# Attention with sinks and a two-matrix gate on one core: a sink tile staged in the gate's buffer, and every piece in a fixed order

## The chip, the cores and the metric

The kernel runs on one core of a Trainium2 chip. The metric is the device time of one execution in microseconds (us), and the reported time is the median over runs. An engine here is one of five: TensorE (PE, with its weight loads shown apart as PEld), VectorE (DVE), ScalarE (ACT), GpSimd (POOL) and SyncE (SP), which only issues DMAs. Each engine works through its own instructions in the order in which they are written; between engines there are semaphores.

## The reference, cut to what matters

```python
scores = matmul(q, k.T) / sqrt(64)                 # batch 4, heads 8, sequence 768, head size 64
keep = (pos_k < n_sink) | ((0 <= pos_q - pos_k) & (pos_q - pos_k < window))   # 4 sinks, window 128
a = softmax(where(keep, scores, -1e9));  x = matmul(a, v)      # -> 3072 tokens x 512
h = x @ w_in                                       # 512 -> 2048
out = (h - tanh(h)) @ w_out                        # 2048 -> 512
```

All inputs are float32. The two matrices come as 64-bit words from which the kernel decodes float32 on the chip.

## The kernel before, in words

The 3072 tokens are cut into 12 chunks of 256 queries (three per batch). The first three chunks are the first ones of batches 0, 1 and 2. Per chunk there are four **units** (a pair of heads each), so 48 units. A unit needs: loads of keys and queries; scores (`products`, L532 for the first twelve units, L539 after them), twice, for two tiles t of 128 queries; `merge` on DVE (L554, L556), which reads the scores out of PSUM; `exponent` on ACT (L564); `sums` on DVE (L584, L585) and `scale` on ACT (L590), which divide; `sinks` on POOL (L599 to L601); and `transposes` on PE (L624) into the PSUM bank t, which ACT (L631) and DVE (L638) copy out into `pts`. When two units (in the first two chunks) or four are done, `attend` makes x of them: `sink_rows` (L665) transposes the sinks' columns, ACT copies them (`sink_copy`, L672), and `values` (L681 with the sinks' values `vsink`, L687 with v) accumulates x, which ACT and DVE split into a high and a low part (L704, L708).

The sinks' values of a batch are made by `sink_values`, seven times in all, whenever the batch changes from one chunk to the next: a DMA (L460) into the tile `vraw`, a rounding copy on ACT into `vsink` (L466), a subtraction and a scaling on POOL in place in `vraw` (L470, L471), and a sum on DVE into `vsink` (L475).

The two matrix products follow in **steps** n = 0 to 95, one for a chunk and an eighth g of the 2048 columns: `first_half(n)` (24 products, L823) makes h; the gate takes tanh on ACT into `gbuf` (L854), the difference on DVE (L857), and a high and a low part (L860, L863; in the later chunks sums and L873, L876); `second_half(n)` multiplies with the second matrix (L905; in the later chunks L939). The weights are decoded once, early: DVE takes three instructions per matrix part (L157, L159, L161), ACT rounds (L747), DVE makes the low part (L751). From step 24 on the first matrix is streamed back from a scratch copy in DRAM into the tiles `ring` and `spare` (L808).

All of this is entered as 3002 **pieces** into one object, `work`: each with its engine, an expected duration, a due time, the function that issues its instructions, and the names that it reads and writes. `Work.order` (L195 to L231) then runs a list scheduler on these numbers: an engine takes, of its ready pieces, the one with the earliest due time. The pieces are issued in the order of their starts in this plan. So the plan fixes only who stands before whom in each engine's queue; the chip's semaphores decide when a piece starts.

## Time and profile before

| what | us |
|---|---|
| median of three runs | 668.6 (666.87 to 668.98) |
| the profiled execution | 670.4 |
| its span, first to last instruction | 668.6 |
| PE busy in it | 650.5 |

The profiled execution is 1.8 us longer than its own span; that part lies outside the instructions. The page's list of engines gives the busy time per engine over the span; windows give the same for a stretch, with the clock that TensorE was granted (1.00 is 2.4 GHz, 0.50 is 1.2 GHz); a timeline gives instructions in order of time, and in brackets how long the engine had stood idle before one and what ended that.

### The profile page before, as it was taken

How to read it: one execution, taken by the hardware profiler on the slowest of the kernel's cores; microseconds unless marked ns; L12 is line 12 of the kernel's file. 1: busy time of each engine (PE TensorE's matmuls, PEld its weight loads, DVE VectorE, ACT ScalarE, POOL GpSimd, SP SyncE). 2: the span in 40 equal slices, each digit the busy share in tenths (PEclk: the TensorE clock that was granted, in tenths of full speed). 3: DMA queues.
4: the chain of work that ended last, by engine and by line, in shares of the span. 5: the costliest groups of instructions: out<-in, count | busy, mean ns of one | idle time of the engine just before them, and what ended most of it. 6: DMA issues, size and time to landing. Idle time of an engine off the chain costs nothing.

```text
span 668.6 us, 14547 instructions
## 1 busy us (share of the span) xinstructions
PE 650.5 (97%) x5099; PEld 603.3 (90%) x5099; DVE 543.8 (81%) x1399; ACT 396.9 (59%) x1024; POOL 164.2 (25%) x331
## 2 busy tenths in 40 slices
PE   6989999999999999999999999999999999999996
PEld 4668899999979899898999999999999999999995
DVE  6889999964999878578798899887899899855654
ACT  5987444345898667567665575676566566523321
POOL 5453100000873232243331212312213212100100
PEclk9899999999999999999999999999999999999999
DMA  5877788884999667899977767767776867656771
GB/s 172 279 254 273 260 268 308 292 289 143 226 212 279 217 205 226 236 291 279 287 221 219 223 208 239 251 185 209 243 221 203 266 182 209 206 165 210 259 199 40
DMA packets 79502, 152.97 MB, mean 229 GB/s; under 512 B 9596, under 2 KB 25852, under 8 KB 79420
## 3 DMA queue, kind: packets, MB, share of 16 engines
q1 hardware_dynamic: 65900, 121.52, 58.3%
q0 software_dynamic: 13376, 30.30, 16.1%
q8 instruction: 42, 0.69, 0.4%
q14 instruction: 40, 0.33, 0.1%
q10 hardware_dynamic: 144, 0.13, 0.1%
HBM read 131.47 MB, written 20.45 MB: 227 GB/s over the span
## 4 chain that ended last, share of the span: by engine, by line
PE 76%; DVE 8%; ACT 6%; DMA 4%; issue 2%; POOL 2%; SPq 0%; POOLq 0%; DVEq 0%; ACTq 0%
PE h L823 33%; PE s L939 10%; PE o L939 7%; PE o L905 6%; PE x L687 3%; PE s L905 3%; PE t L624 2%; PE t L687 2%; DMA kraw<-kp 2%; PE t L539 2%; PE t L905 2%; PE x L905 2%; PE x L539 1%; ACT p L590 1%; DVE pt L638 1%
## 5 line engine op out<-in xcount | busy, mean ns | idle before, releaser
L823 PE MATMUL h<-xall,ring 128*128 128x256 f32 x990 | 130.3, 279 | 0.0
L823 PEld LDWEIGHTS h<-xall,ring 128*128 128x128 f32 x990 | 121.1, 188 | 1.4 <-issue 0.7
L854 ACT ACTIVATE gbuf<-h 128x512 f32<-128x512 f32 x96 | 57.1, 595 | 91.4 <-PE h L823 67.6
L823 PE MATMUL h<-xall,spare 128*128 128x256 f32 x738 | 97.6, 279 | 0.0
L873 ACT CAST ghbuf<-gbuf 128x896 fp32r<-128x896 f32 x55 | 51.7, 940 | 68.5 <-DVE gbuf L870 68.4
L823 PEld LDWEIGHTS h<-xall,spare 128*128 128x128 f32 x738 | 90.9, 188 | 0.5
L370 POOL DMA_DIRECT2D qraw<-qd x36 | 26.6, 740 | 255.8 <-DVE q L511 199.9
L876 DVE TENSOR_TENSOR glbuf<-gbuf,ghbuf 128x896 fp32r<-128x896 f32 x55 | 60.0, 1090 | 20.4 <-ACT ghbuf L873 17.5
L564 ACT ACTIVATE p<-p,st 128x132 f32<-128x132 f32 x132 | 52.4, 399 | 12.9 <-DVE st L556 12.0
L857 DVE TENSOR_TENSOR gbuf<-h,gbuf 128x512 f32<-128x512 f32 x55 | 37.9, 689 | 22.9 <-ACT gbuf L854 22.4
L905 PE MATMUL o<-w,ghbuf 128*128 128x512 f32 x192 | 49.9, 395 | 0.2 <-ACT ghbuf L860 0.2
L823 PEld LDWEIGHTS h<-xall,w 128*128 128x128 f32 x384 | 46.9, 188 | 2.0 <-DVE w L751 0.4
L823 PE MATMUL h<-xall,w 128*128 128x256 f32 x384 | 48.2, 279 | 0.2 <-DVE w L751 0.2
L502 DVE TENSOR_TENSOR ks<-kraw,ks 64x392 fp32r<-64x392 f32 x72 | 40.4, 561 | 5.9 <-ACT ks L497 3.8
L590 ACT ACTIVATE p<-p,st 128x132 f32<-128x132 f32 x132 | 42.6, 395 | 3.1 <-DVE st L585 2.6
L905 PEld LDWEIGHTS o<-w,ghbuf 128*128 128x128 f32 x192 | 33.8, 188 | 6.1 <-ACT ghbuf L860 0.5
L857 DVE TENSOR_TENSOR h<-h,gbuf 128x512 f32<-128x512 f32 x41 | 28.5, 696 | 13.0 <-ACT gbuf L854 12.7
L497 ACT CAST ks<-kraw 64x392 fp32r<-64x392 f32 x72 | 37.1, 515 | 2.2 <-DMA kraw<-kp 1.3
L860 ACT CAST ghbuf<-h 128x512 fp32r<-128x512 f32 x41 | 24.0, 585 | 21.1 <-DVE h L857 20.4
L939 PE MATMUL s<-edge,ghbuf 128*128 128x256 f32 x220 | 35.3, 279 | 0.0
L939 PE MATMUL o<-w,ghbuf 128*128 128x256 f32 x220 | 35.1, 278 | 0.0
L939 PE MATMUL s<-w,ghbuf 128*128 128x256 f32 x220 | 35.1, 278 | 0.0
(185 smaller groups left out, 1546.5 us busy)
## 6 DMA issues: line engine op xcount, KB each, us to landing
ring<-wscr SPq DMA_DIRECT2D x165, 256.0 KB, 4.8
spare<-wscr SPq DMA_DIRECT2D x123, 256.0 KB, 4.7
qraw<-qd POOLq DMA_DIRECT2D x36, 256.0 KB, 5.2
wraw<-w_in SPq DMA_DIRECT2D x16, 512.0 KB, 5.8
wraw<-w_out SPq DMA_DIRECT2D x16, 512.0 KB, 5.6
wscr<-w SPq DMA_DIRECT2D x16, 512.0 KB, 7.4
kraw<-kp POOLq DMA_DIRECT2D x36, 196.0 KB, 4.7
v<-vp POOLq DMA_DIRECT2D x18, 256.0 KB, 3.8
```

What stands on the lines that cost most here:

```text
L497: nc.scalar.copy(ks[u][r, h, :], kt[u][r, :])
L502: (nc.gpsimd if KP else nc.vector).tensor_tensor(k[o, h, :], t[r, :], k[r, h, :].bitcast(F32), op=ALU.subtract)
L564: nc.scalar.activation(e, e, AF.Exp, bias=st[u][:, j : j + 1], scale=-1.0, accum_out=st[u][:, 4 + j : 5 + j],)
L590: nc.scalar.activation(pr[u][:, j, :], pr[u][:, j, :], AF.Copy, scale=s[:, 8 + j : 9 + j])
L687: nc.tensor.matmul(xps[key][(p - p0) // 2][h * 64 : h * 64 + 64, p % 2, a:z], lhsT=vt[cc, i][:, hd : hd + D], rhs=rhs, start=False, stop=p ...
L823: nc.tensor.matmul(hps[n][:, f, :], lhsT=w, rhs=x, start=r == 0, stop=r == 11)
L854: nc.scalar.activation(g0, h(), AF.Tanh)
L857: nc.vector.tensor_tensor(g0 if strassen(n) else h(), h(), g0, op=ALU.subtract)
L873: nc.scalar.copy(ghbuf[:, n % 2], gbuf[:, 1:, :])
L876: nc.vector.tensor_tensor(low7(n), gbuf[:, 1:, :], ghbuf[:, n % 2].bitcast(F32), op=ALU.subtract)
L905: nc.tensor.matmul(sums_of(n, cc, t), lhsT=a[:, f, t * P : (t + 1) * P], rhs=wt[1, g][:, (0, 1, 0)[i], f, :], start=first and not low and ...
L939: nc.tensor.matmul(acc, lhsT=a[:, b, :], rhs=factor(g, m, part % 2), start=g == 0 and part == 0 and m in (4, 1, 2, 7), stop=closes(n) and ...
```

## The change: what it does

Four edits. **The order** of the 3002 pieces is no longer planned: it is a permutation, stored as a compressed string, and `Work.order` unpacks it and asserts that no piece stands before one that it depends on. **The staging**: `sink_values` of batch 1 (the second batch; it is made twice, for the second and for the sixth chunk) uses the first 128 columns of the gate's tile `gbuf` in place of `vraw`, and the name that orders it is the gate's, `"gr"`. **The names**: the copies of the transposes into `pts` now also name the decode buffers that lie in the same memory (`"dw"`), so that the assertion sees them. **ASIDE**: in five steps the low part of the gate's numbers lies at element 4 of its tile, in steps 81, 84, 87, 90 and 93, where it lay at 4 or 44 in steps 81, 83, 86, 89 and 92; all other steps keep 48.

```diff
-    WAKE = {"PE": 250, "ACT": 170, "DVE": 90, "POOL": 100, "SP": 80}
-    def __init__(self, slack, pad, late, land):
+    ORDER = (
+        "c-jrt0|OW~69CZUF1brCwQbwBZQHhO+qP|Et8KemyVb^4uHW~5#nVcuu?o}#WtCGwO;M4QQBl=6HD8TaG1NqbYLX)5)eOaIvYM$D"
...
     def order(self):
-        todo = {}
...
-        return sorted(start, key=lambda n: (start[n], n)), start
+        todo = [n for n, in iter_unpack("<H", decompress(b85decode(self.ORDER)))]
+        at = {n: i for i, n in enumerate(todo)}
+        assert len(at) == len(todo) == len(self.all)
+        assert all(at[a] < at[n] for n in todo for a in self.all[n][4])
+        return todo
...
-        ASIDE = {81: 4, 83: 44, 86: 4, 89: 44, 92: 4}
+        ASIDE = {n: 4 for n in (81, 84, 87, 90, 93)}
...
         def sink_values(b, due):
-            slot = "vraw"
+            slot = "gr" if b == 1 else "vraw"
+            raw_at = gbuf[:, 0, :] if b == 1 else vraw
             def load():
-                nc.sync.dma_start(vraw, vs[32 * b : 32 * b + 32].rearrange("r (p c) -> p r c", c=P))
+                nc.sync.dma_start(raw_at, vs[32 * b : 32 * b + 32].rearrange("r (p c) -> p r c", c=P))
...
-                    nc.scalar.copy(vsink[r, i, :], vraw[r])
+                    nc.scalar.copy(vsink[r, i, :], raw_at[r])
...
-                work.add("ACT", 260, d + 1400, whole, ["t"], [("pt whole", m)])
-            work.add("DVE", 430 if c == 0 else 710, d + 1500, lambda: part(1, below), ["t"], [("pt own", m)])
+                work.add("ACT", 260, d + 1400, whole, ["t"], [("pt whole", m)] + [("dw", m - 2)] * (m > 1))
+            free = [("dw", m - 2)] * (m > 1)
+            work.add("DVE", 430 if c == 0 else 710, d + 1500, lambda: part(1, below), ["t"], [("pt own", m)] + free)
```

What the permutation does to the queues: the first halves keep their order among themselves, the second halves keep theirs, and 33 of the 864 pieces of both stand at another place among the others. From step 86 on (608 us in the profile) PE's queue is the same piece for piece. The attention's pieces move: against the queue before, about one in seven of PE's pieces, and about four in ten of DVE's and ACT's, have another rank among their engine's. Three places follow; line numbers of the changed kernel are some 35 higher (L568 is L532 before, L660 is L624, L702 is L665, L718 is L681, L942 is L905, L575 is L539, L496 is L460).

**PE's queue at the start**, before and then now: `pt` holds keys and queries of units 0 and 1, `kraw,qraw` those of unit 2, `qk` of the later ones; s and o are the PSUM banks of the scores.

```order
L532 MATMUL s_250<-pt 128x260
L532 MATMUL s_251<-pt 128x260
L532 MATMUL o_252<-pt 128x260
L532 MATMUL o_253<-pt 128x260
L532 MATMUL s_250<-kraw_272,qraw_270 128x260
L532 MATMUL s_251<-kraw_272,qraw_270 128x260
L532 MATMUL o_252<-kraw_272,qraw_270 128x260
L532 MATMUL o_253<-kraw_272,qraw_270 128x260
L624 MATMUL t<-ident,p_284 128x128 x4
```

```order
L568 MATMUL s_250<-pt 128x260
L568 MATMUL s_251<-pt 128x260
L660 MATMUL t<-ident,p_291 128x128 x4
L568 MATMUL o_252<-pt 128x260
L568 MATMUL o_253<-pt 128x260
L568 MATMUL s_250<-kraw_304,qraw_276 128x260
L568 MATMUL s_251<-kraw_304,qraw_276 128x260
L568 MATMUL o_252<-kraw_304,qraw_276 128x260
L568 MATMUL o_253<-kraw_304,qraw_276 128x260
```

The four transposes of unit 0 stood behind the scores of unit 2; they now stand behind the first scores of unit 1 and ahead of its second ones.

**SP's queue at the start**, before and then now, from the first DMA behind the branch: `vs` are the sinks' values, `qd` queries, `kp` keys, `vp` values, `w_in` a weight part.

```order
L361 DMA kraw_272<-kp 128x392
L105 DMA qraw_270<-qd 64x256 x2
L405 DMA v_0_289<-vp 128x512
L405 DMA v_1_291<-vp 128x512
L361 DMA qk_287<-kp 128x392
L105 DMA qk_287<-qd 64x256 x2
L460 DMA vraw<-vs 128x1x128
L416 DMA wraw_0_340<-w_in 128x1024
L361 DMA qk_297<-kp 128x392
L105 DMA qk_297<-qd 64x256 x2
```

```order
L496 DMA vraw<-vs 128x1x128
L105 DMA qraw_276<-qd 64x256 x2
L396 DMA kraw_304<-kp 128x392
L396 DMA qk_280<-kp 128x392
L396 DMA qk_282<-kp 128x392
L105 DMA qk_280<-qd 64x256 x2
L451 DMA wraw_0_327<-w_in 128x1024 x2
L105 DMA qk_282<-qd 64x256 x2
L440 DMA v_0_352<-vp 128x512
L440 DMA v_1_354<-vp 128x512
```

The sinks' values of batch 0 are now the first load, and the values of v come behind the keys and queries of units 3 and 4.

**PE's queue at the fourth chunk's x** (190 us), before and then now: `glbuf` is the low part of a gate, `z` the sinks' columns, `zr` their copies.

```order
L624 MATMUL t<-ident,p_2147 128x128 x4
L905 MATMUL o_252<-w_6_1522,glbuf 128x512 x2
L905 MATMUL o_253<-w_6_1522,glbuf 128x512 x2
L665 MATMUL x<-ident,z 128x128 x2
L539 MATMUL s_250<-ks_2225,q_2204 128x260 x2
L539 MATMUL s_251<-ks_2225,q_2204 128x260 x2
L681 MATMUL x<-zr,vsink 128x512
```

```order
L660 MATMUL t<-ident,p_2134 128x128 x4
L702 MATMUL x<-ident,z 128x128 x2
L942 MATMUL o_252<-w_6_1540,glbuf 128x512 x2
L575 MATMUL s_250<-ks_2171,q_2164 128x260 x2
L575 MATMUL s_251<-ks_2171,q_2164 128x260 x2
L942 MATMUL o_253<-w_6_1540,glbuf 128x512 x2
L718 MATMUL x<-zr,vsink 128x512
```

The transposes of the sinks' columns moved ahead of a pair of products with the gate's low part, so that four more products stand between them and the product that reads `zr`.

## Rows read from the trace of the kernel before

**Rows 1.** The page's first part: busy us, share of the span, instructions.
```profile
PE 650.5 (97%) x5099; PEld 603.3 (90%) x5099; DVE 543.8 (81%) x1399; ACT 396.9 (59%) x1024; POOL 164.2 (25%) x331
```
**Rows 2.** Windows: length, busy us (count) of PE, PEld, DVE, ACT, POOL; clock; DMA.
```profile
0.00:60.00 60.00, 50.60 (x292) 38.28 (x293) 48.19 (x206) 46.97 (x173) 30.22 (x77) 0.97 0.73 235
60.00:190.00 130.00, 129.76 (x862) 117.55 (x861) 109.80 (x185) 69.36 (x146) 23.98 (x36) 1.00 0.80 255
190.00:460.00 270.00, 268.15 (x2175) 249.78 (x2174) 227.53 (x631) 180.62 (x484) 81.29 (x159) 1.00 0.79 236
460.00:610.00 150.00, 150.00 (x1339) 146.52 (x1338) 124.73 (x317) 83.77 (x203) 26.03 (x56) 1.00 0.70 212
```
**Rows 3.** PE's timeline in the first 50 us: start, length, what, [idle before it].
```profile
8.11 1.12 PE L532 MATMUL s<-pt 128*128 128x260 f32 x4
...
13.70 1.12 PE L532 MATMUL s<-qk 128*128 128x260 f32 x4 [0.81 <-DMA qk<-qd]
14.65 1.04 PE L532 MATMUL o<-qk 128*128 128x260 f32 x4
17.99 2.07 PE L532 MATMUL s<-qk 128*128 128x260 f32 x4 [2.30 <-DVE nswi L556]
...
49.15 1.77 PE L823 MATMUL h<-xall,w 128*128 128x256 f32 x12
```
**Rows 4.** SP's timeline: issues of the sinks' values, and the issue between them.
```profile
11.19 0.67 SPq L460 DMA_DIRECT2D vraw<-vs  x1
...
15.48 1.11 SPq L105 DMA_DIRECT2D qk<-qd  x2
19.16 0.58 SPq L460 DMA_DIRECT2D vraw<-vs  x1
```
**Rows 5.** ACT's timeline from 9 to 16 us.
```profile
9.79 0.19 ACT L564 ACTIVATION_READ_ACCUMULATOR p<-p,st 128x1 f32 x1
...
10.71 1.29 ACT L590 ACTIVATE p<-p,st 128x132 f32<-128x132 f32 x4
...
15.32 0.62 ACT L466 CAST vsink<-vraw 64x128 fp32r<-64x128 f32 x2 [1.76 <-DMA vraw<-vs]
```
**Rows 6.** DVE's timeline, at 10 to 17 us and at 69 us.
```profile
10.24 0.16 DVE L584 TENSOR_SCALAR st<-st 128x4 f32<-128x4 f32 x1
...
16.88 0.29 DVE L584 TENSOR_SCALAR st<-st 128x4 f32<-128x4 f32 x1 [1.72 <-ACT wide L564]
...
68.80 0.71 DVE L475 SCALAR_TENSOR_TENSOR vsink<-vsink,nswi,vraw 64x128 fp32r<-64x128 f32 x2 [0.27 <-POOL vraw L471]
69.52 2.36 DVE L751 TENSOR_TENSOR w<-pt,w 128x1024 fp32r<-128x1024 f32 x2
```
**Rows 7.** Windows around PE's longest wait, same columns as rows 2.
```profile
14.50:17.90 3.40, 1.19 (x6) 0.69 (x4) 1.47 (x10) 2.53 (x10) 1.27 (x3) 1.00 0.97 318
17.90:21.30 3.40, 3.31 (x11) 2.85 (x12) 2.04 (x11) 3.12 (x14) 0.63 (x3) 0.50 0.43 143
```
**Rows 8.** PE's timeline: its waits behind 60 us.
```profile
70.80 2.40 PE L823 MATMUL h<-xall,w 128*128 128x256 f32 x18 [0.24 <-DVE w L751]
...
194.39 0.50 PE L681 MATMUL x<-zr,vsink 128*128 128x512 f32 x1 [0.75 <-ACT zr L672]
...
209.38 2.11 PE L905 MATMUL o<-w,ghbuf 128*128 128x512 f32 x8 [0.24 <-ACT ghbuf L860]
...
317.78 0.63 PE L624 MATMUL t<-ident,p 128*128 128x128 f32 x3 [0.26 <-ACT p L590]
```
**Rows 9.** The gate of step 33 and its second half: ACT's and PE's timeline.
```profile
268.13 0.58 ACT L854 ACTIVATE gbuf<-h 128x512 f32<-128x512 f32 x1
...
276.80 1.55 PE L905 MATMUL o<-w,ghbuf 128*128 128x512 f32 x6
```
**Rows 10.** POOL's timeline: one making of the sinks' low part.
```profile
238.11 1.01 POOL L470 TENSOR_TENSOR vraw<-vraw,vsink 64x128 f32<-64x128 f32 x2
239.22 0.37 POOL L471 TENSOR_SCALAR vraw<-vraw,nswi 128x128 f32<-128x128 f32 x1
```

More of the change, by code (lines that the diff above doesn't have):

```diff
@@ L179, in __init__ @@
+    def __init__(self):
         self.all, self.wrote, self.read = [], {}, {}
-        self.slack, self.pad, self.late, self.land = slack, pad, late, land
     def add(self, engine, took, due, fn, reads=(), writes=(), lands=0, port=False):
@@ L195, in order @@
     def order(self):
-        todo = {}
-        for n, (engine, *_) in enumerate(self.all):
-            todo.setdefault(engine, []).append(n)
-        users, left = [[] for _ in self.all], [len(t[4]) for t in self.all]
-        for n, t in enumerate(self.all):
-            for a in t[4]:
-                users[a].append(n)
-        ready = {n: 0.0 for n, k in enumerate(left) if k == 0}
-        waiting = {e: [n for n in v if n in ready] for e, v in todo.items()}
-        free, port, start, done = dict.fromkeys(todo, 0.0), {}, {}, {}
-        def at(n, e):
-            t = max(free[e], ready[n])
-            return max(t, port.get("DVE" if e == "POOL" else "POOL", 0.0)) if self.all[n][6] else t
-        while any(waiting.values()):
-            t, e = min((min(at(n, e) for n in v), e) for e, v in waiting.items() if v)
-            n = min((n for n in waiting[e] if at(n, e) <= t), key=lambda n: (self.all[n][2], n))
-            _, took, _, _, _, lands, locks = self.all[n]
-            took *= self.pad if e in ("ACT", "DVE", "POOL") and self.all[n][2] > self.late else 1.0
-            waiting[e].remove(n)
-            start[n], free[e], done[n] = t, t + took, t + took
-            if lands:
-                free[e], done[n] = t + (took if e == "POOL" else lands), t + lands + (1700 if self.all[n][2] < self.late else self.land)
-            if locks:
-                port[e] = t + took
-            for u in users[n]:
-                f = self.all[u][0]
-                lag = 0 if f == e else self.WAKE[e]
-                if f == "PE":
-                    lag += self.slack if self.all[u][2] > self.late else 100
-                ready[u] = max(ready.get(u, 0.0), done[n] + lag)
-                left[u] -= 1
-                if not left[u]:
-                    waiting[f].append(u)
-        return sorted(start, key=lambda n: (start[n], n)), start
+        from base64 import b85decode
+        from struct import iter_unpack
+        from zlib import decompress
+        todo = [n for n, in iter_unpack("<H", decompress(b85decode(self.ORDER)))]
[3 more added lines that the diff above has]
+        return todo
 def _banded(tc, qd, kp, vp, vs, small, masks, w_in, w_out, ident, pts, early, out):
@@ L268, in _banded @@
         SA, NSLOT, RING, GP, LQ, ST = 5, 7, 7, 0, 1, 1
-        work = Work(SLK, PAD, LATE, LAND)
+        work = Work()
         chunks = [(b, 0) for b in range(3)] + [(b, c) for b in range(3) for c in range(1, CPB)]
@@ L475, in total @@
                     nc.vector.scalar_tensor_tensor(
-                        vsink[r, i, :], vsink[r, i, :].bitcast(F32), half[r, 0:1], vraw[r],
+                        vsink[r, i, :], vsink[r, i, :].bitcast(F32), half[r, 0:1], raw_at[r],
                         op0=ALU.mult, op1=ALU.add,
@@ L654, in turn @@
             else:
-                work.add("DVE", 430 if c == 0 else 710, d + 1500, lambda: part(0, after), ["t"], [("pt before", m)])
+                work.add("DVE", 430 if c == 0 else 710, d + 1500, lambda: part(0, after), ["t"], [("pt before", m)] + free)
         def attend(cc, p0, pairs):
@@ L1190, in _banded @@
         second_half(NS - 1)
-        todo, _ = work.order()
+        todo = work.order()
         with tc.manual_schedule(engines={et.PE, et.SP, et.DVE, et.Activation, et.Pool}):
```

68 lines of the change are left out of this document (66 added, 2 removed).

## The prediction

> **What bounds the kernel now.** I read the page's list of engines first: PE is busy for 650.5 of 668.6 us [rows 1], so all that an order can give back is 18.1 us, and only where PE stands. The windows say where that is. In the first 60 us PE is busy for 50.60 and idle for 9.4; from 60 to 190 it is idle for 0.24, from 190 to 460 for 1.85, from 460 to 610 for nothing [rows 2]. The rest lies behind the last product: from step 86 on PE's queue is the same piece for piece, so that tail stays as it is. The clock stands at 1.00 behind 60 us, and at 0.97 on the mean before. What is to be won is therefore nearly all in the first 60 us, and there it is more than PE's own waits: DVE is busy for 48.19 of 60 us, ACT for 46.97, and a lost stretch of DVE comes back as a wait of PE.
>
> PE's timeline shows the two waits that matter early: 0.81 us at 13.70 for a query DMA and 2.30 us at 17.99, and behind the second, four score products take 2.07 us where the same four took 1.12 at 8.11 and 13.70 [rows 3]. The windows on both sides say why: granted clock 1.00 in the 3.4 us of the wait, 0.50 (1.2 GHz) in the 3.4 us behind it, in which PE is busy for 3.31 [rows 7]. At 2.4 GHz that work would have taken about half, so the fall costs up to 1.7 us more. The trace puts the 2.30 us down to a merge (L556), but the busy figures beside it are low for DVE too (1.47 of 3.40), and DMA is at 0.97: the work was late in arriving, not long in being done. SP's timeline shows one reason: the second load into `vraw` (L460) is issued at 19.16, where the issue before it had ended at 16.59 [rows 4]. SP stood for 2.57 us until the first batch's sum had let go of `vraw`, and every load behind it stood too. ACT's shows another: it stops for 1.76 us at 15.32 because its queue holds the rounding of `vraw`, whose DMA was issued at 11.19 [rows 4, 5], and DVE, waiting for ACT's exponents, stops for 1.72 us at 16.88 [rows 6].
>
> **The change part by part.** *Taken away at the start.* The sinks' load goes first in SP's queue, so the 1.76 us of ACT and the 1.72 us of DVE go; the staging in `gbuf`, which no step of the gate uses yet at 17 us, takes away SP's 2.57 us. The keys of the third and fourth unit are issued earlier, so the 0.81 and 2.30 us of PE need not come.
>
> *Added at the start.* Unit 0's transposes now stand ahead of unit 1's second products. They need unit 0's scaled exponents. Before, PE had enough behind them in the queue to cover that; now it has not. The chain from rows: the last pass of unit 0's second tile reads out at 9.79 and takes 0.19, so to 9.98; sums on DVE are two instructions, the first of 0.16 at 10.24; with the hand-overs I put 0.5 for them, to about 10.5; scale on ACT takes 1.29 for four, and if it no longer stands behind unit 1's passes it ends at about 11.8 [rows 5, 6]. The scores at 8.11 end at 9.23 [rows 3]. So PE stands from 9.23 to about 11.88, 2.65 us, at a place where it worked before, and DVE, which has merged what there is, starves for some 2 us behind it.
>
> I followed the four queues by hand from there, with each instruction's duration from the trace before and the new order. Unit 3's second products end at 18.4 us, against 15.69 before (14.65 and 1.04), 2.7 later. But then nothing waits: unit 4's scores follow at once, where before they started at 17.99 and ran at half clock, to 20.06 [rows 3]. DVE at the end of its first weight part is 1.0 late, the queues are level at about 26 us, and ahead from there since ACT's, DVE's and SP's stops are gone. The six products that open step 0 (at 49.15, 1.77 for twelve, so half of it to 50.0 [rows 3]) come out 1.2 us earlier. I take **−1.2** for the start. Its bounds: of PE's waits of 0.81 and 2.30 and the 1.7 of clock nothing new is put in their place, −4.8; and the whole of the new stop with a clock that falls behind it, 2.65 and 1.7, less the 0.81 that is surely gone, +3.5.
>
> The Trainium skill ("TensorE: Matmul & The Clock Gate", section "HAM oscillation — how this bites in real kernels") tells that a wait of the engine for data can throttle the clock, and that the products behind it then start cold. The trace agrees for the wait at 17.99 [rows 7]; by that rule the new stop of 2.65 us would be followed by a stretch at 0.50 too, and the start would come to −1.2 + 1.7 = +0.5 (a rival, below). The row of the 0.81 us wait speaks the other way for short ones: the four behind it take 1.12 [rows 3]. I keep −1.2, because what PE does after the stop is at first little and paced by DVE, so that the clock would cost less than 1.7.
>
> *Behind 60 us.* At 70.80 PE waits 0.24 us for a weight's low part; ahead of that part, which starts at 69.52 on DVE, stands the sum L475 of the sinks' values, 0.71 us [rows 6, 8]. The sum now stands behind it, and DVE comes ahead by about a microsecond: the wait goes, −0.24. At 194.39 it waits 0.75 for the sinks' copies; four more products with the gate's low part now lie between the transposes and the reader (two in front of the scores, two behind), and they take longer than the wait: −0.75. At 209.38 and 317.78 it waits 0.24 and 0.26 [rows 8]; in the new queues what PE waits for has been moved forward on ACT by more than that: −0.50. That the new order has no waits elsewhere I can't read from it. The nearest rows are the small waits themselves; I put in two of them, **+0.5**, with bounds of 0 and of +3 (four like the longest, 0.75).
>
> *The staging in the sixth chunk* puts work into a tile that the gate wants. The load follows the difference of the gate before (about 261 us). Rounding on ACT takes 0.62 [rows 5], the two steps on POOL 1.01 and 0.37 [rows 10], and the sum on DVE 0.71 [rows 6], which stands behind two copies in the queue and ends at about 270.7. The tanh of step 33 ran at 268.13, and it now waits for that. Its product with the second matrix runs at 276.80 [rows 9], and tanh, difference and high part (0.58 and about 0.7 and 0.6) need 1.9 us, so it must start by 274.9: 4.2 us are in hand. Cost nothing; what hides it are the first-half products and the values of that chunk, some 5 us of PE. Behind the waiting tanh on ACT stands the copy of the sinks' columns; if POOL or DVE were 4 us late, PE would wait for the remainder. The new names only serve the assertion, and the place of the low part in its tile in five steps adds no instruction: nothing for both.
>
> The sum: −1.2 − 0.24 − 0.75 − 0.50 + 0.5 = −2.2. The profiled execution, 670.4, would be 668.2 with a span of 666.4; the median of the runs, 668.6, would be **666.4**.
>
> **The rivals.** *Deeper:* PE's stop at 9.23 is filled or is short, and the early loads let everything behind it start at once with the clock at 1.00 throughout. Then the 4.8 us at the start go without one in return, and with the later ones the time is 668.6 − 4.8 − 1.49 + 0.5 = 662.8. For it: DMA's share is 0.97 in the stretch of the wait [rows 7], and the new order puts what is wanted first into that queue. Against it: the transposes' chain of 2.65 us is made of rows, and the total of bytes in the first 60 us is the same. *Clock:* the start does as I say, but the clock stands at 0.50 for the 3.4 us behind the new stop, as in the row behind the old one [rows 7]: +1.7, so 668.1. For it speaks that both stops are of nearly one length; against it, that PE has little to do just then. *Break-even:* the start does as I say, and the middle, in which PE now stands for 2.1 us in 400 [rows 2], gets waits of its own: scores moved ahead of merges that must free their banks, at 161 to 186, 374 to 400 and about 490 us. At the bound of +3 in place of 0.5 the time is 668.9. *Slower:* the new stop at 9.23 is what decides. It takes 2.65 us, the clock falls behind it as it did behind the 2.30 [rows 7], 1.7, and DVE, starved for 2 us, doesn't come level before it has the weights to decode, so that a wait like the one at 17.99 comes again later: +4.35, less the 0.81 at 13.70, less about 1.0 for the waits at 194.39 and 317.78 [rows 8], +2.5, 671.1. It decides if unit 0's transposes start later than about 11.9 and the clock in the 3.4 us behind them is near 0.50. *That the change does not do what it says* I leave at nothing: the queues show the places as told.
>
> **How the numbers follow.** About 0.3%, 2.0 us, is what can be told from no change in this kernel. Forecast (−1 to −3.5): 0.50, some 0.28 of it beyond 2.0 us. Deeper (−3.5 to −7): 0.20. Clock (−1 to +0.5): 0.08. Break-even (−1 to +2): 0.09. Slower (beyond +2): 0.13. So faster 0.28 + 0.20 = 0.48, same 0.22 + 0.08 + 0.09 = 0.39, slower 0.13. The range leaves out a tenth at the fast end (half of the deeper case, below −5.6: 663.0) and somewhat under a tenth at the slow end (two thirds of the slower case, above +2.3: 670.9).
>
> **What would show it.** The start is right if PE stops for 2 to 3 us at about 9.2, if SP, ACT and DVE have no stops at 15 to 19, and if step 0's first products run about 1 us earlier than at 49.15; right in size if PE's busy and idle time up to 60 us tells the same. The later steps are right if the waits at 70.80, 194.39, 209.38 and 317.78 are gone, and step 33's second half does not wait. It is wrong if a stretch at 0.50 follows the stop, if PE's idle time from 60 to 610 is above 3 us, or if what comes early at 49 us is given back before 60, by DVE's decoding of the weights.

## The result: slower by one per cent, outside the range

| | before | changed |
|---|---|---|
| median of 20 runs, us | 668.7 | 676.8 |
| lowest and highest | 666.87 and 670.47 (19 runs) | 671.32 and 679.83 |
| ratio to before, 95% interval | | 1.0104 (1.0084 to 1.0124) |
| profiled execution, and its span | 670.4, 668.6 | 676.75, 675.0 |

I had forecast 666.4 with a range of 663.0 to 670.9; every one of the 20 runs of the changed kernel lies above it. Of the 20 runs of before, 19 lie between 666.9 and 670.5 and one, at twice the time, is left out. The changed kernel's runs fall in two groups with nothing between: eight from 671.3 to 674.2 and twelve from 676.4 to 679.8. The profiled execution is one of the upper group. So there are two things to explain: the 4.6 us between the medians of the groups (672.9 and 677.5), and why even the lower group is some 4 us above before.

The page's first part and the same windows as [rows 1, 2], of the changed kernel (length, busy us and count of PE, PEld, DVE, ACT, POOL; clock; DMA):

```profile
PE 655.8 (97%) x5099; PEld 605.6 (90%) x5099; DVE 548.4 (81%) x1399; ACT 396.8 (59%) x1024; POOL 154.0 (23%) x331
...
0.00:60.00 60.00, 49.22 (x279) 36.92 (x281) 49.45 (x203) 45.05 (x169) 24.89 (x72) 0.94 0.69 218
60.00:190.00 130.00, 128.86 (x850) 115.53 (x847) 108.55 (x181) 67.24 (x140) 20.92 (x35) 1.00 0.77 251
190.00:460.00 270.00, 269.39 (x2160) 249.98 (x2159) 226.08 (x618) 179.47 (x482) 80.14 (x162) 1.00 0.80 237
460.00:610.00 150.00, 149.98 (x1311) 146.93 (x1311) 128.67 (x333) 86.75 (x212) 25.47 (x61) 1.00 0.71 219
```

These rows mislead whoever reads idle time alone. From 60 to 610 us PE is idle for 1.77 us, less than the 2.09 of before, and yet it does less in the same time: 1311 matmuls in the last window against 1339. PE's busy time over the span rose from 650.5 to 655.8 with the same 5099 instructions. The clock explains little of that: pool_restored (below), whose clock doesn't fall in the first 60 us, still has 654.7. The ends of the products are modelled in the profile, so a short stop can be shown as busy time. The measure that doesn't mislead is the start of the same piece. For six pieces of the two products, the set of PE's pieces ahead of them is the same in all kernels of this study, so what their start differs from before is time lost (+) or gained (−). The table is worked out from the traces of the profiled executions, in us; the times at its head are those of before.

| kernel | step 0, 49.15 | step 16, 143.79 | step 37, 294.29 | step 56, 418.02 | step 80, 572.15 | last, 661.40 |
|---|---|---|---|---|---|---|
| changed | +2.32 | +1.20 | +3.18 | +4.31 | +6.49 | +6.37 |
| pool_restored | −2.43 | −3.55 | −1.55 | −0.33 | +1.77 | +1.91 |
| head_before | −0.83 | −0.81 | −0.84 | +0.68 | +2.64 | +2.82 |
| head_after | +2.13 | +1.01 | +10.73 | +9.94 | +9.93 | +9.20 |
| head_restored | −1.99 | −3.25 | −3.10 | −4.70 | −4.54 | −5.03 |
| before_staged_once | −1.09 | −1.09 | −1.01 | −2.43 | −2.25 | −2.98 |
| late_only | −0.36 | −0.38 | +0.10 | +1.66 | +5.32 | +4.95 |
| late_swaps | −1.17 | −1.17 | −1.06 | +1.33 | +6.81 | +8.15 |
| u13_back | −2.00 | −3.11 | −0.74 | +0.54 | +2.21 | +2.79 |
| mid | −1.98 | −3.24 | −1.44 | −0.07 | +0.21 | −0.14 |
| transposes_back | −1.25 | −2.51 | −2.27 | −3.44 | −3.21 | −3.17 |

The names are those of the runs below. Each row compares two single executions, and those of one kernel differ: the 19 runs of before by 3.6 us, and its profiled one, 670.4, is 1.7 above their median. So the table tells where time is lost more surely than how much, and it shows losses too small and gains too large against a median run of before; where a size matters, the medians decide.

### The profile page after: what moved, and what is told of

It reads as the page before. It is cut to its first block, busy times and chain, and to the rows that moved or that the text cites. A ratio compares the mean times of both kernels' runs of the same rounds, so it can differ in the third digit from the quotient of the medians.

```text
span 675.0 us, 14510 instructions
## 1 busy us (share of the span) xinstructions
PE 655.8 (97%) x5099; PEld 605.6 (90%) x5099; DVE 548.4 (81%) x1399; ACT 396.8 (59%) x1024; POOL 154.0 (23%) x331
## 4 chain that ended last, share of the span: by engine, by line
PE 85%; DVE 4%; ACT 3%; DMA 2%; issue 2%; POOL 1%; SPq 1%; POOLq 0%; ACTq 0%; DVEq 0%
PE h L860 37%; PE s L976 11%; PE o L942 10%; PE o L976 8%; PE x L724 3%; PE s L942 3%; PE t L660 3%; PE t L724 2%; PE s L575 2%; PE t L575 2%; PE x L575 2%; DMA kraw<-kp 2%; PE t L942 1%; PE x L942 1%; DMA v<-vp 1%
## 5 line engine op out<-in xcount | busy, mean ns | idle before, releaser
L405 POOL DMA_DIRECT2D qraw<-qd x36 | 28.1, 780 | 149.9 <-DVE q L547 124.2
L396 POOL DMA_DIRECT2D kraw<-kp x36 | 20.6, 572 | 132.8 <-DVE ks L538 84.5
L942 PE MATMUL o<-w,ghbuf 128*128 128x512 f32 x192 | 49.8, 396 | 0.0
L942 PEld LDWEIGHTS o<-w,ghbuf 128*128 128x128 f32 x192 | 33.9, 188 | 6.3 <-issue 0.3
```

Of the source, the lines that this page charges most:

```text
L942: nc.tensor.matmul(sums_of(n, cc, t), lhsT=a[:, f, t * P : (t + 1) * P], rhs=wt[1, g][:, (0, 1, 0)[i], f, :], start=first and not low and ...
```

## The profile after: the start

DVE's and POOL's timelines of before from 4.7 us (start, length, engine, line, what, [idle before it]):

```profile
4.76 0.51 DVE L136 TENSOR_SCALAR pt<-pt,nswi 128x4 f32<-128x4 f32 x1
...
7.72 0.30 DVE L556 CUSTOM_DVE_ANT_0 p<-s,mask 128x132 f32<-128x132 f32 x1 [2.06 <-POOL qk L377]
```
```profile
4.72 0.53 POOL L377 MEMSET qraw<- 128x512 f32 x1 [1.47 <-issue]
5.19 0.21 POOL L444 IOTA nswi<- 128x2 int32 x2
```

The same two of the changed kernel:

```profile
4.76 3.99 DVE L136 TENSOR_SCALAR pt<-pt,nswi 128x4 f32<-128x4 f32 x1
8.78 0.16 DVE L137 TENSOR_TENSOR pt<-pt 128x4 f32<-128x4 f32 x1
8.98 0.16 DVE L138 TENSOR_TENSOR mask<-pt 128x4 f32<-128x4 f32 x1
11.29 0.30 DVE L592 CUSTOM_DVE_ANT_0 p<-s,mask 128x132 f32<-128x132 f32 x1 [2.15 <-issue]
```
```profile
4.74 0.21 POOL L479 IOTA nswi<- 128x2 int32 x2 [1.50 <-issue]
4.89 0.32 POOL L480 MEMSET vsink<- 128x256 f32 x1
5.14 0.32 POOL L481 MEMSET z<- 128x256 f32 x1
5.39 0.53 POOL L412 MEMSET qraw<- 128x512 f32 x1
...
5.86 2.87 POOL L412 MEMSET qk<- 128x512 f32 x6
```

L136 is an instruction of 128x4 numbers that makes the mask. It takes 3.99 us here and 0.51 in before, and it ends at 8.75, when POOL's run of memsets ends (5.86 and 2.87: 8.73). In before POOL's queue had the memset of `qraw` first and the iota second; the change swapped the two, so that nine memsets now follow the iota without anything between. I had not looked at this pair. The first merge (L592; L556 in before) starts 2.06 to 2.18 us behind the end of L138 in 15 of the 16 traces of this study, and 2.60 in one (u13_back). So it comes at 11.29 in place of 7.72, and PE, whose next scores need a bank that the merge must read first, stands until then:

```profile
6.81 1.32 PE L568 MATMUL o<-pt 128*128 128x260 f32 x4
11.65 2.10 PE L568 MATMUL s<-pt 128*128 128x260 f32 x4 [3.52 <-DVE st L592]
14.51 1.49 PE L660 MATMUL t<-ident,p 128*128 128x128 f32 x4 [0.76 <-ACT p L626]
```

In the windows around it the granted clock is 0.89 in the stop and 0.50 in the 3.4 us behind it, as it was behind the 2.30 us of before [rows 7]; the whole stretch at 0.50 lasts from 10.8 to 17.6 us, and PE is busy for 5.1 us of it, so that the clock costs up to 2.5 us here (an estimate: half of that):

```profile
8.00:11.60 3.60, 0.13 (x1) 0.00 (x0) 1.39 (x6) 0.00 (x0) 0.72 (x2) 0.89 0.61 179
11.60:15.00 3.40, 2.58 (x5) 1.36 (x5) 2.23 (x16) 2.81 (x12) 0.00 (x0) 0.50 0.70 207
15.00:18.00 3.00, 2.90 (x9) 2.44 (x10) 0.82 (x4) 2.03 (x10) 1.89 (x6) 0.57 0.86 308
```

## Experiments on the start

All kernels of this study compute the whole reference. They are the changed kernel with another list of pieces and, where said, with the staging in the gate's tile for the second chunk only or for none; "the order of before" means its list of pieces, with the changed kernel's names and ASIDE. PE's, DVE's, ACT's, POOL's and SP's queues follow from the list.

**pool_restored.** POOL's pair alone is put back.

```diff
-POOL: IOTA nswi, MEMSET vsink, MEMSET z, MEMSET qraw, MEMSET qk x6
+POOL: MEMSET qraw, IOTA nswi, MEMSET vsink, MEMSET z, MEMSET qk x6
```

> The changed kernel with one pair swapped in POOL's queue: the memset of qraw stands again ahead of the iota and the two memsets of the sinks' constants, as it did before. Theory P: the mask instruction L136 on DVE (0.51 us before, 3.99 us after) stands while POOL's memsets run one behind the other; with the old order it takes about 0.5 us, the first merge starts at about 7.7 instead of 11.29, PE's 3.52 us stop shrinks below 1 us or moves to unit 0's transposes (about 2 to 3 us), and step 0's first products start 3 us or more earlier than at 51.47. Time about 672 (range 670 to 674). Rival T: the start is lost because unit 0's transposes stand ahead of unit 1's second products, whatever L136 does: L136 gets short but step 0 still starts at 51 and the time stays at 676 to 677.

Measured: 672.4 (8 runs, 671.8 to 673.8), 1.0046 of before (1.0030 to 1.0062). The upper group is gone, and what is left is like the lower group (672.9). The clock of the single runs fits: its mean over a run is 0.989 to 0.993 in all twelve of the changed kernel's upper group, and 0.997 to 0.999 in all eight of the lower and in these eight. So the fall of the clock belongs to the upper group. DVE's, POOL's and PE's timelines of this run:

```profile
4.76 0.52 DVE L136 TENSOR_SCALAR pt<-pt,nswi 128x4 f32<-128x4 f32 x1
...
7.75 0.30 DVE L592 CUSTOM_DVE_ANT_0 p<-s,mask 128x132 f32<-128x132 f32 x1 [2.08 <-POOL qk L412]
```
```profile
4.73 0.53 POOL L412 MEMSET qraw<- 128x512 f32 x1 [1.48 <-issue]
5.20 0.21 POOL L479 IOTA nswi<- 128x2 int32 x2
```
```profile
8.52 1.40 PE L568 MATMUL s<-pt 128*128 128x260 f32 x4
10.97 0.33 PE L660 MATMUL t<-ident,p 128*128 128x128 f32 x1 [1.05 <-ACT p L626]
11.56 0.62 PE L660 MATMUL t<-ident,p 128*128 128x128 f32 x3 [0.26 <-ACT p L626]
```

L136 ends at 5.28, just behind the start of the iota at 5.20. PE's stop at the transposes is 1.05 and 0.26 us, the clock stays at 1.00 through 22 us, and step 0 comes 2.43 us ahead of before, 4.75 ahead of the changed kernel's profile. By step 16 it is 3.55 ahead. So theory P holds and T falls: POOL's pair cost 4.75 us in the profiled execution, and the transposes' place doesn't decide.

**before_pool_swapped.** The same pair swapped the other way in the order of before (without any staging).

```diff
-POOL: MEMSET qraw, IOTA nswi, MEMSET vsink, MEMSET z, MEMSET qk x9
+POOL: IOTA nswi, MEMSET vsink, MEMSET z, MEMSET qraw, MEMSET qk x9
```

> The order of the kernel before, with only POOL's pair swapped the other way, as in the changed kernel: iota and constants ahead of the memset of qraw. Theory P: L136 takes some 3.5 to 4.5 us (until the run of memsets on POOL ends), the first merge starts at 11 or later, and the time rises by 3 to 6 us over the 668.7 of before, to 672 to 675. Rival T: L136 may be long, but the time stays within 1 us of 668.7.

Measured: 670.9, 1.0033 (1.0012 to 1.0053), between what I expected and the rival; but the ten runs divide again, five at 669.2 to 670.0 and five at 671.8 to 673.5. In the profiled one, of the lower half (670.02), L136 took 0.22 us. So with the swap alone half of the runs are late, by about 3 us; that L136 is long in them is likely but not shown, since none of them was profiled.

**pool_longer.** Three more of the changed kernel's own memsets are moved up into the run.

```diff
-POOL: ..., MEMSET qk x6, CAST z, ...
+POOL: ..., MEMSET qk x9, CAST z, ...
```

> The changed kernel with three more of its own memsets of qk moved up into the run of six on POOL (nine in a row, as before had, about 1.4 us more). Theory P: where L136 on DVE is caught it now lasts until the longer run ends, about 5.4 us in place of 3.99, and these executions take about 678 to 679; where it is not caught nothing changes, 671 to 674. Rival: L136 waits for something else (its data, its code), and stays at 3.99 or below.

Measured: 679.1 (two runs at 673.8 and 674.0, four at 678.8 to 680.3), 1.0162 (1.0146 to 1.0177). The upper group is higher by 1.9 than the changed kernel's (median 679.4 against 677.5), the lower by 1.0 (673.9 against 672.9). The profiled run was of the lower group, with L136 at 0.22; how long it takes when it is caught is not shown.

**pool_sure.** The constants stand behind the run of seven memsets, so that the run starts POOL's queue.

```diff
-POOL: IOTA nswi, MEMSET vsink, MEMSET z, MEMSET qraw, MEMSET qk x6
+POOL: MEMSET qraw, MEMSET qk x6, IOTA nswi, MEMSET vsink, MEMSET z
```

> The changed kernel with the iota and the constants of the sinks moved behind the run of seven memsets on POOL, so that the run starts at 4.7 us, when L136 on DVE is issued, and nothing else stands in it. Theory P (L136 cannot start while memsets follow one another on POOL): L136 is caught in every execution, lasts until the run's end at about 8.1 us (about 3.3 us in the profile), and all executions lie in the slower group that the changed kernel has, 676 to 679, none below 675. Rival (chance, or something that the iota does): L136 0.2 to 0.5 us and times of 671 to 674 in some or all executions.

Measured: four runs at 676.3 to 679.4 and one at 671.3. I had expected no such run. It is the profiled one, and its DVE and POOL timelines tell why:

```profile
4.75 0.22 DVE L136 TENSOR_SCALAR pt<-pt,nswi 128x4 f32<-128x4 f32 x1
```
```profile
5.24 0.53 POOL L412 MEMSET qraw<- 128x512 f32 x1 [2.00 <-issue]
5.70 2.83 POOL L412 MEMSET qk<- 128x512 f32 x6
```

Here DVE came first, took 0.22, and it was POOL that started late, at 5.24 in place of 4.73. Over the 16 traces the rule has no exception. Where POOL's first instruction there starts at 4.72 to 4.75, 10 to 40 ns ahead of L136, L136 takes 0.51 to 0.55 if a single memset and then the iota stand first (eight traces), and 3.99 if the iota and then the run do (the changed kernel and head_after). In the six traces where POOL starts at 4.80 or later, L136 takes 0.22. With so few ns between them I take it that each execution decides anew who is first, and that the order of POOL's queue decides what it costs when POOL is: the two groups of times agree with that. The five profiled executions of kernels with the run at the head lie where they should, two with 3.99 in the upper group and three with 0.22 in the lower one. An execution of the changed kernel's own lower group was not profiled; pool_sure and pool_longer, which start step 0 2.11 and 1.79 us ahead of before, are the nearest to it. That four runs of pool_sure are late although the iota stands behind the memsets says that it takes no iota.

The Trainium skill ("SBUF — State Buffer", section "Who interferes with whom") says that DVE and POOL share a port pair, that whoever issues first holds it for its whole instruction, and that a scalar operation of DVE can be of the kind that needs it. The traces agree with both orders, 3.99 and 0.22 us; that it is this port is what the skill says, no run here tells it from something else that the two engines share. What the traces add is that a row of memsets let L136 in at none of its joints, while it got in where an iota followed the first memset.

**transposes_back.** From head_restored (below), unit 0's four transposes go back behind unit 2's scores on PE.

```diff
-PE: scores u1 (t0), transposes u0, scores u1 (t1), scores u2
+PE: scores u1 (t0), scores u1 (t1), scores u2, transposes u0
```

> The run with the changed kernel's start, POOL's pair restored and the later order of before (665.4), with unit 0's four transposes put back behind unit 2's scores on PE. Where they stand now PE stops for 1.05 and 0.26 us. Theory A: that stop is on the path, and the time falls by 0.5 to 1.3 us, to 664.2 to 664.9. Theory B: PE is ahead of DVE there anyway, the stop moves to the next wait: 665.1 to 665.7. Theory C: later readers of the transposes (the copies of unit 0) become late: 666 or more.

Measured: 665.9 (10 runs), 0.9960 (0.9946 to 0.9974), against 665.4 and 0.9957 of head_restored: no gain, so theory A falls. The time lies between the ranges of B and C, and the trace shows what B says: the stop only moves. With the transposes out of the way PE waits for unit 2's keys, which the changed order loads behind the sinks' values:

```profile
11.59 1.12 PE L569 MATMUL s<-kraw,qraw 128*128 128x260 f32 x4 [1.56 <-DMA kraw<-kp]
```

**before_staged_once.** The order of before, with the staging for the second chunk.

```diff
-slot = "vraw"
+stage = b == 1 and due < 50000
+slot = "gr" if stage else "vraw"
```

> The order of before, piece for piece, with the staging in the gate's tile for the second chunk alone. SP no longer stands behind the second load of the sinks' values (19.16 before), ACT's 1.76 us and DVE's 1.72 us stops at 15 to 17 us stay, because the first load keeps its place. If the staging is worth something by itself: 0.5 to 1 us at step 0, time 667.7 to 668.5. If the loads behind it were not what PE waited for: 668.7 to 669.3.

Measured: 668.9 (10 runs), 1.0008 (0.9996 to 1.0020). The profiled execution is 1.09 us ahead at step 0, but it was the shortest of the ten (667.53); the median shows nothing. By itself the staging is worth nothing that can be told here, as the second expectation had it.

## Experiments on the later steps

**head_after and head_before.** One list up to a piece of step 16 (590 pieces of the changed list, or 594 of before's), the other behind it.

```diff
-order = changed
+order = changed[:590] + [n for n in before if n not in changed[:590]]    # head_after
+order = before[:594] + [n for n in changed if n not in before[:594]]     # head_before
```

> The changed kernel's order for the pieces up to about 145 us, the order of before for all later ones. In the traces the changed kernel is 1.2 us late at 73 to 157 us and 6.4 us late at the end. Theory two places (the start costs 1 to 2 us in the profiled runs, the small waits behind 157 us about 5): 669.5 to 671.5. Rival one place (the start is all, the later delay follows from it): 674 to 677.

> The order of before for the pieces up to about 145 us, the changed kernel's for all later ones. Theory two places: 672.5 to 674.5, with PE's new stops at about 165 to 168 us (ks of unit 13, 1.4 us) and the small ones behind 340 us all there, and no run above 675. Rival one place: 667.5 to 669.5.

In both, the sixth chunk's load of the sinks' values, which before issues into `vraw` at 129.43, stands later than the lists say, where the gate's tile is free.

Measured: head_before 674.7, 1.0107 (1.0063 to 1.0150), so the later part costs by itself: 5.5 us in the median, 3.6 in the table. That is somewhat more than I expected (672.5 to 674.5, none above 675): two of the four runs lie above 675, at 675.4 and 679.0, and for the last I have no explanation. head_after 680.1, 1.0147 (1.0099 to 1.0195), outside both expectations, and not for the reason tested: the delay grows by 9.7 between steps 16 and 37, at one place, a stop of 7.46 us and products at a clock of 0.50 until 276.4. PE's, ACT's and SP's timelines of head_after:

```profile
272.54 1.35 PE L575 MATMUL s<-ks,q 128*128 128x260 f32 x4 [7.46 <-DVE nswi L592]
```
```profile
260.76 0.59 ACT L891 ACTIVATE gbuf<-h 128x512 f32<-128x512 f32 x1
268.08 0.62 ACT L502 CAST vsink<-gbuf 64x128 fp32r<-64x128 f32 x2 [6.72 <-DMA gbuf<-vs]
```
```profile
262.12 0.60 SPq L496 DMA_DIRECT2D gbuf<-vs  x1
```

That is the price of the staging in the sixth chunk where the order makes no room for it: the load can be issued only when the gate is done with the tile, it takes 6 us to land, the rounding that waits for it blocks ACT for 6.72 us, DVE waits behind ACT and PE behind DVE. In the changed kernel the same load is issued at 263.10 and the same rounding runs at 268.00, but the order has put other work of ACT between; ACT's timeline there shows a wait of 0.91 us, the tanh of step 33 follows at 274.90, and its second half starts at 279.60 without a wait:

```profile
268.00 0.62 ACT L502 CAST vsink<-gbuf 64x128 fp32r<-64x128 f32 x2 [0.91 <-DMA gbuf<-vs]
...
274.90 0.60 ACT L891 ACTIVATE gbuf<-h 128x512 f32<-128x512 f32 x1
```

**head_restored.** The changed start with POOL's pair restored, the later order of before, and the sixth chunk's making left in `vraw`.

```diff
-order = before
+order = changed[:590] with POOL's pair restored + the rest of before; staging for the second chunk only
```

> The changed kernel's order up to about 145 us with POOL's pair restored (qraw's memset first), the order of before for all later pieces, and the sinks' values staged in the gate's tile for the second chunk only (the sixth chunk's making uses vraw, as before). Theory two places: the start is worth what the run with POOL's pair restored showed, 3.5 us ahead of before from 76 to 157 us, nothing is given back later, and the time is 664.5 to 666. Rival: whatever the start gains the later steps lose, since their transfers and copies are timed for the slower start: 668 to 670.

Measured: 665.4 (five runs, 665.3 to 665.7), 0.9957 (0.9943 to 0.9970): faster than both kernels. What the start gains is kept: 3.6 us in the medians. The 5.03 of the table's last column compares it with an execution of before that is 1.7 above the median; 1.0 of it arises between steps 40 and 42, where before waits at 317.78 [rows 8] and this run does not.

**late_only.** The order of before up to 327 us, the changed one behind it.

```diff
-order = before
+order = before[:1489] + [n for n in changed if n not in before[:1489]]; staging for the second chunk only
```

> The order of before up to about 327 us, the changed kernel's for all later pieces, sixth chunk staged as before. Theory many small stops: the late part alone brings its own, 3.5 to 4.5 us behind 340 us, mostly second halves that wait for the gate's high part and scores that wait for a merge, each with about 0.11 us behind it; time 672.5 to 673.5. Rival: the late stops follow from what is already late or early in the middle (157 to 340 us), and without it they are below 1 us: 668.5 to 669.8.

Measured: 674.3, 1.0083 (1.0067 to 1.0100). The late part costs 4.9 us by itself between steps 37 and the end (5.3 in the medians), a little more than I expected, and the rival falls. The stops are many and small; the largest of them on PE, and what ACT did before it:

```profile
503.01 0.74 PE L977 MATMUL s<-edge,ghbuf 128*128 128x256 f32 x4 [0.46 <-ACT ghbuf L911]
```
```profile
501.60 0.52 ACT L534 CAST ks<-kraw 64x392 fp32r<-64x392 f32 x1 [1.19 <-DMA kraw<-kp]
502.02 0.94 ACT L911 CAST ghbuf<-gbuf 128x896 fp32r<-128x896 f32 x1
```

The gate's high part stands behind the rounding of a later unit's keys, whose DMA has not landed. How close things run can be counted: for the second-half pieces between 330 and 612 us, the time from the end of their own high or low part on ACT or DVE to their start has a median of 2.12 us in before and 1.53 in late_only, and is below 0.5 us for 2 of 270 and for 27 of 264. (The expectations count a little otherwise and tell the same.)

**late_gate6 and late_swaps.** Two attempts to give it back, both from late_only: all 273 pieces of the gate six places earlier in the list (since they all move, each passes one to five others), or twelve swaps of neighbours in ACT's and DVE's queues at eleven stops.

```diff
+for every piece of the gate behind 327 us: place in the list − 6           # late_gate6
```
```diff
-ACT: rounding of unit 42's keys, high part of step 67
+ACT: high part of step 67, rounding of unit 42's keys
...
-ACT: high part of step 78, scale of unit 46
+ACT: scale of unit 46, high part of step 78
```

> The run with the late part alone (674.3), with the gate's pieces on ACT and DVE behind 327 us moved up by six places in the list of pieces, about 1.3 us. In the late part alone 31 of 232 second-half pieces start less than 0.5 us after their gate part is ready (4 in before). Theory: the second halves wait because the gate's parts stand too far back in ACT's and DVE's queues; with them moved up fewer than 15 stand so close, and the time falls to 670 to 672.5. Rival: what stands ahead of them (keys' DMAs, merges) only waits in another place, and PE with it: 673.5 to 676.

> The run with the late part alone (674.3, 5.3 us over before), with twelve swaps of neighbours in DVE's and ACT's queues and nothing else: at eleven of its stops of PE behind 340 us, the piece that PE waited for (a sum or a high or low part of the gate, a merge, a copy of transposes, a scale) goes ahead of the one piece that stood just before it in its queue. The eleven stops are 0.12 to 0.63 us, 3.4 in all, each with about 0.11 behind it. Theory queue place (the stops come from pieces that stand one place too far back): 2 to 4 us come back, 670.3 to 672.3. Rival (DVE and ACT have no slack there, and a swap only makes the other piece late): 673.3 to 676.

Measured: 703.2, 1.0532 (1.0500 to 1.0564), and 678.7, 1.0141 (1.0124 to 1.0158). Both theories fall, and both kernels are slower than even the rivals allowed (676). late_gate6 does what it was to do: by the count above the second halves have 2.11 us in hand again, with 9 of 240 below 0.5. But now other pieces come late, and PE stands for them; the two longest entries among its waits behind the start-up (us in total, times, longest):

```profile
PE t L576 <- DVE pt L675: 6.5, 8, 1.8
PE t L661 <- ACT p L627: 3.9, 10, 0.9
```

Scores wait for the copy of transposes (L675), transposes for the scale (L627). So it is not the second halves alone that have nothing in hand. In late_swaps too each stop that was mended has another beside it: the scale of unit 46, now first, waits 1.04 us for DVE, the high part behind it comes late, and PE stands for more than it did:

```profile
571.99 1.29 ACT L627 ACTIVATE p<-p,st 128x132 f32<-128x132 f32 x4 [1.04 <-DVE st L622]
573.19 0.92 ACT L911 CAST ghbuf<-gbuf 128x896 fp32r<-128x896 f32 x1
```
```profile
574.16 0.74 PE L977 MATMUL s<-edge,ghbuf 128*128 128x256 f32 x4 [1.75 <-ACT ghbuf L911]
```

**u13_back.** From pool_restored, the two scores of unit 13 on PE go back behind the first half of step 20. Before that, the changed kernel's longest waits behind 60 us:

```profile
167.40 0.51 PE L575 MATMUL s<-ks,q 128*128 128x260 f32 x2 [0.59 <-DVE ks L538]
168.42 0.51 PE L575 MATMUL s<-ks,q 128*128 128x260 f32 x2 [0.52 <-DVE ks L538]
```
```diff
-PE: scores u13 (t0), first half of step 20, scores u13 (t1), high part of step 19's second half, transposes u12
+PE: first half of step 20, scores u13 (t0), high part of step 19's second half, transposes u12, scores u13 (t1)
```

> The run with POOL's pair restored (672.4), with the two scores of unit 13 on PE (about 162 us) put back behind the next step's first half, as before. Theory: the 1.44 us that PE waits there for the split of that unit's keys is the cost of having moved them forward, and 1.2 to 1.7 us come back: 670.7 to 671.3. Rival: DVE and ACT, not PE, set the pace from there to 190 us, and the same delay shows up at the scores of units 14 and 15: 671.8 to 673.

Measured: 673.3, 1.0067 (1.0044 to 1.0091), against 672.4 and just above the rival's 673: nothing comes back. The wait for the keys is gone, and the gate's high parts and the later scores wait in its place.

**mid.** The changed order up to 330 us with POOL's pair restored, before's behind it.

```diff
-order = before
+order = changed[:1498] with POOL's pair restored + the rest of before
```

> The changed kernel's order up to about 330 us with POOL's pair restored and both stagings in the gate's tile, the order of before for all later pieces. From the run with POOL's pair restored: 2.4 us ahead at 330 us, 0.8 to 1.1 less than the start alone, since the scores of unit 13 wait 1.4 us for a split at about 162 us and the fourth chunk's wait of 0.9 is gone. If the late steps keep what they get: 665.8 to 667. If the staging in the sixth chunk, which cost 7.5 us of PE in another order, were what makes the later steps late: 670 or more.

Measured: 670.9, 1.0032 (1.0019 to 1.0044), where the second expectation had it (670 or more), but not for its reason. At step 37 it is 1.44 ahead, as pool_restored is; between steps 37 and 56, around the seam at 330 us, it loses 1.37, where head_restored, with before's list there too, gains 1.60; from step 56 to 80 it keeps what it has. Nine of the first 1498 pieces of before's list come late at the seam only because two lists meet there, so this run doesn't tell what the middle alone would cost. Nor does the table's last column tell all here: behind the start of the last product the profiled execution needs 8.4 us, before's 7.2.

## Why the prediction was wrong

**What held.** ACT's, DVE's and SP's stops of before at 15 to 19 us are gone, unit 3's second products end at 18.11 in pool_restored where I had 18.4, and the four waits of [rows 8] are gone: no row of the changed kernel has one for the weight at 70.80, for the high part of step 24, or for the scale of unit 27, and the reader of `zr` at 196.86 follows without idle time. The staging in the sixth chunk costs PE no wait, as said, though with less in hand than I had put: the sum on DVE ends at 274.43, not at about 270.7. That it was the order that made it so, head_after shows with 7.46 us.

**The first step that failed** is the term of −1.2 for the start, at "I followed the four queues". POOL's was among them only for what it hands on, not for what stands beside DVE: the pair that the change swaps there was in no term. With the pair as changed, and POOL first, the term is +2.32 at step 0 and +1.20 at step 16. With the pair restored it is −2.43 and −3.55, with the transposes' stop at 1.31 where I had 2.65, and no fall of the clock. The forecast lies between the two and describes neither. Within it the chain to the transposes was right up to the scale, which I put at about 10.5; it then waited for the scale's end, which PE doesn't. ACT's timeline of pool_restored:

```profile
10.51 1.29 ACT L626 ACTIVATE p<-p,st 128x132 f32<-128x132 f32 x4 [0.51 <-DVE nswi L484]
```

The first transpose runs at 10.97, 0.46 behind the start of these four, and the other three from 11.56.

**The rival named *Slower*** gave PE's stop, 0.50 behind it and DVE starving, and all three are in the profile (3.52 us, 0.50, merges 3.57 late). Its cause was another, so its test "unit 0's transposes start later than 11.9" is met (14.51) for a reason that I didn't name. The 1.7 us for the clock, which stands in my bounds and in three of the rivals, was read from one execution. Other executions, of kernels that start with before's list but for one small edit, have such a stop without a fall: before_pool_swapped 2.83 us, before_staged_once 2.12. PE's timeline of before_pool_swapped, and the windows of its stop and behind it (as rows 2):

```profile
18.57 1.11 PE L568 MATMUL s<-qk 128*128 128x260 f32 x4 [2.83 <-DVE o L590]
```
```profile
15.70:18.60 2.90, 0.07 (x2) 0.06 (x1) 0.67 (x4) 2.25 (x9) 1.28 (x3) 1.00 0.96 319
18.60:22.00 3.40, 2.62 (x14) 1.96 (x14) 3.22 (x14) 3.40 (x16) 1.26 (x6) 1.00 0.16 53
```

**The second step that failed**, and the larger one, is +0.5 for new waits behind 60 us, with a bound of +3. From step 16 to the end the changed kernel loses 5.17 us net, though it also sheds the four waits, 1.49 by my own sum: some 6.7 us of new delay. The medians agree: pool_restored and head_restored share their start, and the later order, with the sixth chunk's staging, makes 672.4 out of 665.4. The bound came from the waits of before, four of its longest. Nothing in that says how many there may be: a trace of before can't show a wait that only the new order has. What I could have counted is the time in hand before each second half, 2.12 us in the median of before; with four pieces in ten of ACT and DVE at another rank, moves of one or two pieces of 0.5 to 1.3 us use that up, as late_only shows. But late_gate6 shows that this count alone doesn't tell the time: it has 2.11 and is slower by 35 us than before.

**The test that I named failed too.** I had said that above 3 us of idle time from 60 to 610 would show the later steps wrong. They are wrong with 1.77.

**What stays open** is which queue of the late part takes its time in hand away, and what in the middle (steps 16 to 37, where pool_restored loses 2.0) costs what it does: mid, the run for it, has the seam's own loss in it. The three attempts to give time back (late_gate6, late_swaps, u13_back) only moved the stops; that all of DVE and ACT is to blame, rather than one early cause, is argued from that and not shown. How long L136 lasts with the longer run wasn't caught in a profile.

## What to carry to other kernels

When an order of pieces changes, go through every engine's queue for what it runs beside, not only for whom it hands on to: a swap of two set-up instructions on POOL cost 4.6 us in three runs of five. Count the time in hand before each instruction of the busiest engine in the trace of before, of all its kinds and not of one, since an order that uses it up turns into stops that the idle time doesn't show; compare the starts of the same pieces. Take no price from a single execution when others of the same kernel differ by more than that price. Keep the part of a change that gains: the start of this one, with POOL's pair and the sixth chunk's staging as before, and the old order behind it are 0.43% faster than before.

## What the runs showed of the hardware that I had not expected

- A DVE instruction on 128x4 numbers stood for 3.99 us while nine memsets followed one another on POOL, though each of these is 0.3 to 0.5 us; with an iota behind the first memset it stood for 0.51 to 0.55.
- In ten traces POOL's instruction started 10 to 40 ns ahead of that of DVE, in six it started 30 to 490 ns behind it, L136 took 0.51 to 0.55 or 3.99 us where POOL was first, by what stood next in POOL's queue, and 0.22 where it was not. The changed kernel's two groups of times, 672.9 and 677.5 in the median, agree with its falling either way from one execution to the next.
- The length of a stop of PE alone doesn't say whether the clock falls. Stops of 2.30 us (before), 3.52 (the changed kernel), 7.46 (head_after) and 1.52 (late_gate6, 0.50 from 501.0 to 504.3) were followed by 0.50, and so were two of 1.56 and 1.78, 2.4 us apart (transposes_back, 0.50 from 17.4 to 20.7); stops of 2.83 (before_pool_swapped) and 2.12 (before_staged_once) left it at 1.00, and so did 1.05 and 0.26 (pool_restored). The Trainium skill ("TensorE: Matmul & The Clock Gate", section "HAM oscillation — how this bites in real kernels") tells that a wait can throttle the clock, and the traces agree with "can".
- Many short stops of PE have about 0.11 us more shortly behind them, at one of the next twelve instructions: counted from start to start behind 150 us, 14 of the 15 stops of the changed kernel that are above 0.12 us, and 4 of 7 in before.
